# A hand-written order of 2159 steps, searched anew with copies tied to a load

## The chip, the cores and the metric

The kernel runs on one core of one Trainium2 chip. The metric is the device time of one execution in microseconds (us). The core's engines are TensorE (PE in the profile, its weight loads PEld), VectorE (DVE), ScalarE (ACT), GpSimd (POOL) and SyncE (SP), which here issues nearly all DMA transfers.

## What is computed

A recurrent attention with a decaying state, and behind it a gated product with a short convolution. Cut to what matters:

```python
# r, k, v, w: (4, 8, 768, 48) float32; u: (8, 48)
for t in range(S):
    cur = np.einsum('bhd,bhe->bhde', u[None] * kt, vt)
    y[:, :, t] = np.einsum('bhd,bhde->bhe', rt, state + cur)
    state = wt[:, :, :, None] * state + np.einsum('bhd,bhe->bhde', kt, vt)
# x: y as (4, 768, 384); w_in (384, 1024), w_out (1024, 384), three-row conv_w (float64)
h = np.maximum(x @ w_in, 0.0)
conv_out = sum(conv_w[j] * shifted(h, j - 1) for j in range(3))
out = (h * sigmoid(conv_out)) @ w_out
```

## The kernel before

The sequence is cut into 24 chunks of 128 times (four batches of six). For each chunk `loads` (L568) brings w, k and r into "nat" tiles and v into "v" tiles. TensorE transposes them, for chunks 8 to 23 in two rounds named 'f1' and 'f2' (L779). VectorE's scans (L645, L653) and products make the operands "kr". For chunks from 4 on, six small DMAs per chunk, the "spreads" (L674), lay out rows of kr for two more heads. `stage_b` (L716) computes scores, on TensorE, masks them (L795, VectorE) and forms the chunk's output y.

From chunk 8 on a chunk is split in two halves of 64 times. Its v goes by two loads (L581) into two of four v tiles, 64 rows each: the first tile holds v of the first half in rows 0 to 63, the second that of the second half in rows 64 to 127. The other rows of the same tiles take a copy of the state, so that one product yields what comes from inside the half and from the state before it: 'vsa' (L744) copies the decayed state into rows 64 to 111 of the first tile, 'vsb' (L885) the state at the half's boundary into rows 0 to 63 of the second. On TensorE the steps of such a chunk are 'hstate' (L877, needs v), 'hscores' (L763, kr), and 'hy' (L847, all of v, copies and scores); 'hy' is the last reader of a v tile, which is then free for a later chunk's load.

The eight blocks of 384 rows of the second part are on TensorE 'in' steps (L895, three matmuls each) and 'out' steps (L924, three each); between them ScalarE, VectorE and GpSimd form the gate (L907 to L917). ScalarE copies an output (L952) into a strip, SyncE sends it. The weights come in large loads and are converted on VectorE, ScalarE and GpSimd (L476 to L496) in the first 100 us.

Nothing of this is issued in the order of the code. Each step is noted by `op` (L187) with its engine, what it reads, what it writes and what buffers it holds. The list ORDER then gives the order in which `issue` (L205) emits the 2159 steps; each engine runs its own steps in this order. A negative number emits one warm-up matmul (L444) on a free bank. PLACES gives the buffer that a tile takes, at its first step. From what a step reads and writes `op` makes a set of steps that must be issued earlier; `issue` asserts it. Semaphores aren't set by it: they are derived from the memory that the emitted instructions touch.

The numbers of the steps that are spoken of:

| step | what it is |
|---|---|
| 696; 959, 1781, 1829 | y of chunk 7; 'hy' of chunks 10, 20, 21 |
| 788, 1162, 1990 | 'hstate' of chunks 9, 12, 22 |
| 723, 724; 938, 939; 986, 987; 1808, 1809; 1974, 1975 | loads of v, first and second half, of chunks 9, 11, 12, 22, 23 |
| 1146 to 1148; 1191 to 1193 | loads of w, k, r of chunks 13 and 14 |
| 969 to 974; 1134 to 1139; 2005 to 2010 | spreads of chunks 11, 12, 23 |

Of the kernel before, what the change touches and what calls it, by code (L numbers as in the profile page):

```python
# [28 lines left out]
    1, 5, 2, 49, 3, 212, 8, -6, 11, 219, 53, 50, 54, 10, 51, 258, 13, 52, 15, 180, 7, 6, 9, -8, -8, -8, -8, 19, 14,  # L29
    216, 220, 18, 16, 20, 23, 24, 173, 177, 181, 222, 25, 224, 183, 227, 0, 185, 214, 213, -5, -5, -5, 21, 217, 218,  # L30
    223, 228, 22, 165, 225, 188, 232, 26, 233, 166, 175, 174, 234, 167, 179, 251, 255, 259, 189, 229, 178, 190, 17,
    12, 4, 55, 226, 184, 186, 27, 29, 28, 170, 168, 236, 197, 230, 182, 221, 58, 193, 194, 195, 235, 196, 253, 252,
    261, 191, 169, 72, 66, 263, 73, 266, 257, 171, 172, 231, 198, 67, 256, 65, 56, 57, 192, 71, 199, 59, 237, 262,
    60, 267, 268, 61, 264, 242, 243, 203, 205, 215, 176, 30, 408, 271, 272, 74, 200, 68, 206, 207, 204, 201, 260,
    187, 69, 202, 269, 208, 273, 44, 415, 32, 38, 45, 33, 244, 209, 62, 63, 75, 239, 412, 31, 238, 270, 70, 451,
    409, 410, 210, 245, 416, 246, 254, 453, 452, 274, 76, 34, 432, 278, 433, 418, 211, 281, 282, 458, 37, 43, 240,
    413, 241, 455, 275, 414, 276, 35, 277, 420, 283, 247, 419, 459, 424, 248, 279, 457, 39, 461, 423, 434, 456, 265,
    280, 46, 463, 425, 421, 249, 284, 286, 287, 462, 467, 288, 47, 64, 77, 96, 250, 285, 289, 466, 464, 475, 476,
    40, 85, 477, 79, 468, 86, 436, 334, 335, 336, 345, 346, 347, 36, 48, 437, 438, 422, 417, 41, 84, 337, 338, 460,
    348, 349, 103, 429, 607, 431, 426, 428, 427, 430, 611, 647, 469, 609, 473, 608, 411, 470, 454, 472, 474, 471,  # L40
    115, 646, 42, 435, 87, 478, 301, 323, 312, 290, 615, 313, 302, 324, 325, 314, 291, 292, 303, 90, 88, 78, 439,
    616, 80, 89, 81, 104, 339, 105, 91, 350, 92, 351, 352, 340, 341, 110, 614, 353, 617, 342, 111, 442, 619, 98,
    622, 99, 444, 326, 315, 82, 445, 446, 443, 93, 83, 106, 441, 327, 94, 440, 109, 343, 112, 293, 95, 447, 328, 97,
    107, 316, 317, 479, 113, 354, 480, 612, 481, 304, 108, 294, 305, 114, 100, 631, 344, 632, 482, 367, 368, 369,
    448, 484, 483, 318, 329, 319, 306, 320, 295, 653, 485, 486, 613, 330, 331, 101, 720, 725, 449, 450, 650, 487,
    648, 134, 356, 357, 618, 623, 332, 122, 296, 488, 624, 297, 651, 298, 123, 321, 620, 358, 333, 355, 102, 322,
    654, 655, 359, 360, 511, 512, 299, 116, 370, 371, 489, 522, 490, 513, 514, 523, 491, 656, 124, 307, 117, 361,
    118, 125, 308, 670, 119, 300, 362, 676, 681, 363, 658, 372, 309, 373, 364, 661, 126, 120, 652, 524, 533, 534,
    535, 500, 501, 657, 536, 374, 365, 375, 502, 310, 128, 376, 135, 525, 621, 503, 121, 127, 662, 555, 556, 557,
    659, 129, 663, 130, 136, 137, 142, 633, 143, 675, 626, 610, 629, 677, 630, 678, 674, 366, 311, 131, 138, 377,  # L50
    537, 504, 492, 493, 132, 141, 144, 133, 538, 494, 539, 558, 559, 139, 540, 465, 140, 495, 505, 560, 496, 506,
    561, 679, 145, 515, 562, 507, 497, 516, 541, 526, 508, 563, 517, 146, 634, 671, 712, 713, 527, 672, 388, 389,
    390, 391, 392, 398, 399, 400, 401, 402, 393, 403, 404, 394, 405, 635, 395, 378, 379, 406, 636, 680, 509, 637,
    518, 519, 685, 686, 380, 688, 566, 567, 568, 381, 382, 383, 627, 668, 625, 669, 665, 667, 722, 721, 726, 564,
    727, 664, 666, 150, 628, 771, 528, 529, 498, 714, 700, 701, 704, 530, 702, 705, 396, 569, 690, 689, 570, 699,
    571, 572, 770, 573, 638, 732, 384, 385, 640, 733, 735, 639, 641, 649, 769, 693, 711, 708, 709, 710, 706, 707,
    574, 749, 642, 750, 753, 751, 542, 775, 510, 565, 673, 761, 762, 520, 521, 543, 682, 499, 386, 703, 736, 643,
    776, 774, 737, 644, 748, 531, 684, 683, 687, 544, 545, 546, 754, 927, 694, 729, 645, 692, 780, 781, 691, 740,
    783, 695, 696, 547, 548, 660, 723, 983, 988, 549, 763, 741, 915, 550, 916, 744, 919, 917, 920, 937, 942, 697,
    698, 551, 552, 575, 743, 784, 785, 914, 742, 758, 760, 756, 935, 755, 757, 759, 724, 936, 715, 532, 728, 764,  # L60
    718, 717, 719, 777, 765, 768, 716, 766, 984, 941, 778, 730, 940, 553, 985, 767, 554, 975, 976, 928, 576, 1140,
    587, 588, 589, 577, 578, 579, 788, 734, 782, 580, 789, 739, 792, 787, 590, 591, 738, 946, 779, 731, 745, 786,
    947, 790, 791, 746, 990, 752, 747, 793, 794, 949, 795, 963, 964, 965, 951, 950, 962, 989, 592, 593, 851, 967,
    977, 968, 929, 852, 594, 595, 853, 840, 994, 995, 841, 997, 807, 842, 808, 809, 407, 925, 922, 921, 923, 387,
    1192, 773, 1241, 854, 855, 856, 857, 1128, 858, 1129, 859, 1132, 843, 844, 845, 1130, 796, 797, 798, 581, 818,
    819, 820, 582, 583, 938, 926, 772, 930, 973, 1148, 924, 943, 934, 931, 933, 932, 987, 1240, 971, 970, 1146, 974,
    1147, 969, 596, 1133, 1139, 972, 810, 999, 1246, 846, 1137, 1135, 397, 1153, 811, 799, 800, 998, 1127, 847, 812,
    821, 801, 802, 848, 813, 1151, 803, 804, 954, 955, 958, 948, 918, 822, 953, 823, 952, 584, 1152, 945, 966, 957,
    814, 860, 585, 873, 874, 875, 876, 815, 1183, 991, 1184, 978, 979, 861, 1141, 982, 980, 981, 1154, 1155, 824,
    956, 877, 992, 825, 1002, 1157, 1003, 1171, 829, 862, 830, 863, 864, 831, 826, 816, 944, 959, 805, 1159, 1245,  # L70
    1158, 865, 866, 849, 1005, 1172, 878, 1173, 1175, 1142, 1176, 867, 879, 868, 832, 1197, 1004, 939, 1134, 1193,
    1138, 1182, 1191, 1136, 1181, 986, 993, 833, 869, 1170, 996, 597, 598, 599, 600, 601, 602, 603, 604, 1000, 834,
    870, 1001, 1185, 835, 817, 850, 960, 827, 828, 1143, 806, 1144, 1231, 1196, 880, 961, 881, 836, 1198, 837, 1232,
    1145, 1279, 1280, 1006, 1202, 1203, 1007, 1008, 1162, 1163, 1166, 605, 1205, 1156, 1219, 1220, 1223, 1221, 1224,
    1161, 1160, 1064, 1020, 1021, 1065, 1066, 1042, 1022, 1239, 1179, 1177, 1233, 1165, 1206, 1218, 1244, 1207,
    1164, 1067, 1288, 838, 1068, 1287, 882, 1293, 1250, 1167, 1251, 1253, 1168, 1254, 1131, 151, 1169, 1267, 1268,
    1269, 1271, 1255, 1222, 1023, 1024, 1043, 1044, 1009, 1053, 1054, 1055, 1010, 1069, 1272, 1031, 1011, 1289,
    1195, 1228, 1227, 1230, 1180, 1455, 1229, 1194, 586, 1178, 1454, 1226, 1453, 1278, 1225, 839, 1234, 871, 872,
    1186, 1045, 1292, 152, 1046, 1056, 1174, 1057, 1012, 1013, 1266, 1070, 1071, 1294, 1025, 1047, 1026, 1058, 1281,
    1014, 1072, 1059, 1048, 1015, 1032, 1075, 1033, 1076, 1034, 1077, 1027, 1459, 1060, 1049, 1460, 1078, 1035,  # L80
    1061, 1050, 1028, 1036, 1016, 1079, 1017, 1237, 883, 1236, 894, 895, 896, 897, 898, 899, 900, 1189, 901, 902,
    1235, 1190, 1188, 1277, 1275, 1274, 1150, 1149, 1210, 1273, 156, 606, 1276, 1199, 1187, 1037, 1211, 1080, 1214,
    1204, 1081, 1208, 1209, 1258, 1247, 1259, 1051, 1038, 1201, 1200, 1062, 1212, 1248, 1213, 1270, 1249, 1082,
    1039, 1083, 1262, 884, 885, 886, 887, 888, 1215, 1298, 1299, 1252, 1301, 889, 890, 891, 1040, 1216, 1018, 1260,
    1302, 1261, 1458, 1303, 892, 1063, 1445, 1243, 1502, 1503, 1501, 893, 1242, 1446, 1295, 1238, 1282, 1286, 1285,
    1284, 1283, 1052, 1019, 1447, 1217, 1256, 1257, 1433, 1434, 1437, 1435, 1438, 1432, 904, 905, 906, 1263, 1300,
    1464, 1264, 1296, 1507, 1508, 1304, 1305, 1465, 1265, 907, 1086, 908, 1467, 1306, 909, 910, 1087, 1088, 911,
    1084, 1480, 157, 1481, 1307, 1482, 1310, 1485, 1483, 1486, 1469, 1468, 1297, 1309, 1308, 1089, 1506, 1090, 1311,
    912, 1312, 1444, 1441, 1440, 1443, 1442, 1290, 1439, 1291, 1658, 1493, 1494, 1041, 1495, 1448, 1659, 1461, 1450,
# [938 lines left out]
```

## Time and profile before

| | us |
|---|---|
| median of three runs | 332.43 |
| the three runs | 331.68, 332.43, 334.64 |
| the profiled execution, its device time | 334.06 |
| its span, from the first to the last instruction | 331.9 |

The profiled execution is one of its own, not one of the three. Its device time is 2.2 us longer than the span that its trace covers. In the profile an engine's busy time is the union of its instructions; matmuls are pipelined and their ends modelled. A row of the timeline gives in brackets how long the engine was idle before it and what ended that. The chain of work that ended last is followed back from the last instruction; each of its pieces lies between one release and the next.

### The profile page before, as it was taken

The numbers are of one execution on the slowest core, as the hardware profiler recorded it, in microseconds if no ns is written. First come the engines' busy times: TensorE is split into PE (matmuls) and PEld (weight loads), VectorE is DVE, ScalarE is ACT, GpSimd is POOL, SyncE is SP. The second block draws the span as 40 slices with busy tenths as digits, with TensorE's granted clock in tenths as the row PEclk, the third lists the DMA queues.
The fourth block names the chain that finished last, engine by engine and source line by source line (L and its number), as shares of the span: only waits on it lengthen the run. The fifth ranks groups of instructions, "written<-read, shape, count | busy, mean of one in ns | idle before, by whom it ended". The sixth has DMA issues, their size and how long they took to land.

```text
span 331.9 us, 11314 instructions
## 1 busy us (share of the span) xinstructions
PE 315.7 (95%) x4450; PEld 292.6 (88%) x4450; DVE 258.9 (78%) x524; ACT 232.0 (70%) x621; POOL 207.3 (62%) x283
## 2 busy tenths in 40 slices
PE   7999999999999998799999999999999799999994
PEld 5887887989988997799988999998999699999994
DVE  5999998999996997768988997789878677554600
ACT  4458797998766588638966877877577578865531
POOL 5959998899786529645599661596384542334330
PEclk9999999999999999969999999999999899999999
DMA  7999769727555651454545664555416700000014
GB/s 152 247 231 212 246 131 227 178 51 196 106 100 119 139 121 32 93 112 95 147 120 115 136 173 102 149 152 114 83 35 196 200 8 2 2 0 1 2 71 148
DMA packets 114079, 39.36 MB, mean 119 GB/s; under 512 B 102605, under 2 KB 109542, under 8 KB 114022
## 3 DMA queue, kind: packets, MB, share of 16 engines
q1 hardware_dynamic: 114020, 38.59, 48.4%
q8 instruction: 36, 0.59, 0.8%
q14 instruction: 21, 0.17, 0.2%
q10 hardware_dynamic: 2, 0.00, 0.0%
HBM read 31.88 MB, written 4.72 MB: 110 GB/s over the span
## 4 chain that ended last, share of the span: by engine, by line
PE 56%; DVE 15%; DMA 11%; SPq 6%; ACT 5%; POOL 3%; issue 3%; DVEq 0%; ACTq 0%; POOLq 0%
PE bank L924 23%; PE bank L895 17%; PE bank L847 4%; SPq L674 4%; PE bank L779 4%; DMA nat<-in_k_dram 4%; DMA v<-in_v_dram 3%; DVE strip L911 3%; PE bank L763 3%; PE bank L877 3%; DVE strip L909 2%; DVE strip L914 2%; DMA gh<-in_moe_w_out_dram 2%; DMA kr<-kr 2%; DVE kr L645 1%
## 5 line engine op out<-in xcount | busy, mean ns | idle before, releaser
L895 PE MATMUL bank<-xT,wi 128*128 128x386 f32 x576 | 114.6, 349 | 0.2 <-DVE xT L856 0.2
L924 PE MATMUL bank<-wo,gh 128*128 128x384 f32 x576 | 109.2, 340 | 0.4 <-DVE strip L493 0.4
L895 PEld LDWEIGHTS bank<-xT,wi 128*128 128x128 f32 x576 | 103.4, 194 | 2.5 <-DVE xT L856 0.4
L917 POOL TENSOR_TENSOR gh<-strip,gh 128x384 fp32r<-128x384 f32 x64 | 64.9, 1023 | 63.1 <-ACT gh L916 54.2
L924 PEld LDWEIGHTS bank<-wo,gh 128*128 128x128 f32 x576 | 99.5, 188 | 2.0 <-DVE strip L493 0.7
L909 DVE SCALAR_TENSOR_TENSOR strip<-bank,cw,strip 128x384 f32<-128x384 f32 x64 | 38.4, 610 | 16.8 <-ACT strip L908 16.3
L913 ACT ACTIVATE strip<-strip 128x384 f32<-128x384 f32 x64 | 32.5, 522 | 20.5 <-DVE strip L911 20.0
L914 DVE TENSOR_TENSOR strip<-bank,strip 128x384 f32<-128x384 f32 x64 | 34.2, 552 | 8.0 <-ACT strip L913 7.9
L911 DVE SCALAR_TENSOR_TENSOR strip<-bank,cw,strip 128x384 f32<-128x384 f32 x64 | 38.3, 612 | 1.7 <-DVE strip L914 0.9
L908 ACT ACTIVATE strip<-bank,cw 128x384 f32<-128x384 f32 x64 | 36.5, 579 | 2.9 <-DMA out_dram<-strip 0.8
L795 DVE COPY_PREDICATED pm<-upper,bank 128x512 f32<-128x512 int32 x48 | 34.3, 736 | 2.9 <-PE bank L763 1.4
L907 ACT ACTIVATE bank<-bank 128x386 f32<-128x386 f32 x64 | 30.4, 478 | 8.1 <-PE bank L895 7.6
L916 ACT CAST gh<-strip 128x384 fp32r<-128x384 f32 x64 | 31.8, 508 | 3.8 <-DVE strip L914 2.6
L677 POOL TENSOR_TENSOR strip<-nat,nat 128x384 f32<-128x384 f32 x24 | 24.4, 1015 | 13.9 <-DMA out_dram<-strip 5.1
L683 POOL TENSOR_SCALAR_AFFINE_SELECT pm<-dg 128x1024 f32<-128x1024 f32 x24 | 26.7, 1113 | 9.3 <-DVE dg L680 4.8
L605 ACT COPY nat<-nat 128x96 f32<-128x96 f32 x72 | 18.5, 269 | 18.5 <-DMA nat<-in_w_dram 8.7
L692 POOL COPY pm<-kr 48x256 f32<-48x256 f32 x60 | 23.7, 395 | 6.4 <-DMA kr<-kr 3.5
L847 PE MATMUL bank<-pm,v 128*32 128x64 f32 (+3 forms) x1280 | 26.0, 231 | 0.6 <-POOL strip L679 0.6
L847 PEld LDWEIGHTS bank<-pm,v 128*32 128x32 f32 (+2 forms) x1280 | 22.2, 109 | 3.6 <-POOL strip L679 1.0
L679 POOL TENSOR_TENSOR strip<-strip,ubc 128x384 f32<-128x384 f32 x24 | 24.2, 1010 | 0.9
L645 DVE TENSOR_TENSOR_SCAN kr<-bank,one_end 128x387 f32<-128x387 f32 x24 | 23.0, 958 | 1.7 <-PE bank L779 0.8
L653 DVE TENSOR_TENSOR_SCAN kr<-bank,dA 128x387 f32<-128x387 f32 x24 | 23.0, 959 | 0.2
(105 smaller groups left out, 444.2 us busy)
## 6 DMA issues: line engine op xcount, KB each, us to landing
gh<-in_moe_w_out_dram SPq DMA_DIRECT2D x5, 1152.0 KB, 5.8
nat<-in_w_dram SPq DMA_DIRECT2D x24, 192.0 KB, 3.6
nat<-in_k_dram SPq DMA_DIRECT2D x24, 192.0 KB, 3.3
nat<-in_r_dram SPq DMA_DIRECT2D x24, 192.0 KB, 3.3
gh<-in_moe_w_in_dram SPq DMA_DIRECT2D x4, 1152.0 KB, 7.2
out_dram<-strip SPq DMA_DIRECT2D x24, 192.0 KB, 2.1
v<-in_v_dram SPq DMA_DIRECT2D x32, 96.0 KB, 3.1
kr<-kr SPq DMA_DIRECT2D x120, 16.1 KB, 2.4
```

What stands on the lines that cost most here:

```text
L795: op("DVE", "cp", lambda g=g: nc.vector.copy_predicated(out=pm.t[:, g], mask=upper.unsqueeze(1).to_broadcast([P, NP, L]), data=sc[g].t.rea ...
L847: nc.tensor.matmul(rows(a, 32)[:, ts], lhsT=lhs, rhs=rhs, start=((halved or c == 0) and i == 0), stop=(i == count - 1), skip_group_check=True)
L895: nc.tensor.matmul(t.t[:, 0:xs.stop - xs.start], lhsT=wi[:, m, a, f * P:(f + 1) * P], rhs=xT[:, x0 + m, c, xs], start=(m == 0 and j == 0), ...
L907: ("ACT", "relu", lambda: nc.scalar.activation(out=h(0, width + 2), in_=h(0, width + 2), func=AF.Relu), [t], [t]),
L908: ("ACT", "mul", lambda: nc.scalar.mul(out=a(), in_=h(1), mul=cw[:, 1, fs]), [t, "cw"], [a1]),
L909: ("DVE", "stt", lambda: nc.vector.scalar_tensor_tensor(out=a(), in0=h(0), scalar=cw[:, 0, fs], in1=a(), op0=ALU.mult, op1=ALU.add), [t], ...
L911: ("DVE", "stt", lambda: nc.vector.scalar_tensor_tensor(out=a(), in0=h(2), scalar=cw[:, 2, fs], in1=a(), op0=ALU.mult, op1=ALU.add), [t], ...
L913: ("ACT", "sig", lambda: nc.scalar.activation(out=a(), in_=a(), func=AF.Sigmoid), [], [a1]),
L914: ("DVE", "gate", lambda: nc.vector.tensor_tensor(out=g.t[:, 0:width], in0=h(1), in1=a(), op=ALU.mult), [t, a1], [g]),
L916: ("ACT", "cast", lambda: nc.scalar.copy(out=part(0)[:, 0:width], in_=g.t[:, 0:width]), [g], [key]),
L917: ("POOL", "lo", lambda: nc.gpsimd.tensor_tensor(out=part(1)[:, 0:width], in0=g.t[:, 0:width], in1=part(0)[:, 0:width].bitcast(F32), op=AL ...
L924: nc.tensor.matmul(acc.t[:, 0:DM], lhsT=part(a)[:, tt * P:(tt + 1) * P], rhs=wo[:, f, c, :], start=(f == 0 and a + c == 0), stop=(f == FT ...
```

## The change

ORDER and PLACES are replaced as a whole. ORDER has the same 2159 steps in another order and 29 warm-up matmuls instead of 8; all of the 29 stand ahead of the output product of chunk 5. Two steps change in what they are noted to read: the copies 'vsa' and 'vsb' now read the v tile that they write into, where they only held its buffer before. Cut to the core, with those lines of ORDER in which the steps spoken of stand (each line is one of many):

```diff
 ORDER = [
...
-    783, 695, 696, 547, 548, 660, 723, 983, 988, 549, 763, 741, 915, 550, 916, 744, 919, 917, 920, 937, 942, 697,
...
-    1147, 969, 596, 1133, 1139, 972, 810, 999, 1246, 846, 1137, 1135, 397, 1153, 811, 799, 800, 998, 1127, 847, 812,
...
-    956, 877, 992, 825, 1002, 1157, 1003, 1171, 829, 862, 830, 863, 864, 831, 826, 816, 944, 959, 805, 1159, 1245,
-    1158, 865, 866, 849, 1005, 1172, 878, 1173, 1175, 1142, 1176, 867, 879, 868, 832, 1197, 1004, 939, 1134, 1193,
-    1138, 1182, 1191, 1136, 1181, 986, 993, 833, 869, 1170, 996, 597, 598, 599, 600, 601, 602, 603, 604, 1000, 834,
...
-    1540, 1541, 1781, 1829, 1582, 1583, 1429, 1584, 1959, 1411, 1962, 1957, 1960, 1958, 159, 2007, 1421, 2010, 2006,
-    2005, 2008, 1809, 1961, 2009, 1782, 1783, 1576, 1577, 1830, 1542, 1578, 1602, 1585, 1586, 1831, 1543, 1544,
-    1430, 1843, 2019, 2021, 1545, 2020, 1876, 1877, 1878, 1844, 1845, 1974, 1808, 1990, 1966, 1537, 2014, 1979,
...
+    521, 762, 573, 531, 532, 687, 643, 693, 692, 691, 695, 696, 547, 644, 548, 748, 752, 574, 697, 694, 763, 645,
...
+    863, 864, 1241, 1159, 939, 1004, 956, 959, 1158, 993, 876, 1175, 1176, 865, 1005, 866, 1131, 877, 1170, 823,
...
+    1964, 1965, 1543, 1586, 1827, 1574, 2019, 1781, 1829, 1782, 1830, 2020, 1426, 1427, 1428, 1429, 1961, 1960,
+    1957, 162, 1958, 1421, 2008, 1959, 2010, 2007, 2006, 1962, 1809, 1808, 2005, 1974, 2009, 2021, 1587, 1588, 1783,
...
 ]
...
                     op("ACT", "vsa", lambda g=g, p=p: nc.scalar.copy(
-                        out=vN[0].t[HL:HL + D, :, 64 * g:64 * g + D], in_=sd.t[p]), [sd], [(vN[0], 1 + g)], [vN[0]])
+                        out=vN[0].t[HL:HL + D, :, 64 * g:64 * g + D], in_=sd.t[p]), [sd, vN[0]], [(vN[0], 1 + g)])
...
             op("ACT", "vsb", lambda g=g: nc.scalar.copy(
-                out=vN[1].t[0:64, :, 64 * g:64 * g + D], in_=mid.t[64 * g:64 * g + 64]), [mid], [(vN[1], 1 + g)], [vN[1]])
+                out=vN[1].t[0:64, :, 64 * g:64 * g + D], in_=mid.t[64 * g:64 * g + 64]), [mid, vN[1]], [(vN[1], 1 + g)])
```

SyncE's own queue, taken out of the two lists at the places spoken of (v, nat and spread with the chunk's number):

| place | before | after |
|---|---|---|
| from the first to the last load of v 9 | v 9 (723), nat 12, nat 11, three spreads 9, nat 11, three spreads 9, v 9 (724) | v 9 (723), two spreads 9, v 9 (724) |
| around load 939 | v 11 (939), spread 12, nat 14, spreads 12 and 13, nat 14, spreads 12 and 13, v 12 (986) | v 11 (939), spread 12, output, spread 12, nat 14, spread 12, nat 14, spread 12, nat 14, output, two spreads 13, nat 15, spread 12, v 12 (987), v 12 (986) |
| around load 1808 | v 22 (1809), spreads 22 and 23, v 23 (1974), v 22 (1808) | v 22 (1809), v 22 (1808), spread 23, v 23 (1974) |

Load 939 takes the v tile that 'hy' of chunk 10 frees in the order before, the tile that 'hy' of chunk 9 frees in the order after. The two loads of chunk 12 wait for 'hy' of chunk 10 in the order after, those of chunk 22 both for 'hy' of chunk 20; before, 1808 waits for 'hy' of chunk 21.

## Rows read from the trace of the kernel before

**Rows 1.** The page, its first part: busy us, share of the span, instructions

```profile
PE 315.7 (95%) x4450; PEld 292.6 (88%) x4450; DVE 258.9 (78%) x524; ACT 232.0 (70%) x621; POOL 207.3 (62%) x283
```

**Rows 2.** Stretches: length, busy us (instructions) per engine, granted clock, DMA share, GB/s

```profile
9.00:100.00 91.00, 87.75 (x1215) 78.93 (x1214) 88.00 (x181) 71.14 (x203) 80.34 (x94) 1.00 0.72 174
100.00:164.00 64.00, 59.80 (x960) 55.21 (x961) 52.10 (x103) 45.64 (x128) 37.23 (x53) 0.95 0.48 100
164.00:250.00 86.00, 85.60 (x1485) 79.58 (x1479) 72.69 (x143) 62.99 (x173) 55.81 (x76) 1.00 0.50 122
250.00:268.00 18.00, 15.94 (x338) 15.06 (x331) 13.68 (x27) 10.98 (x25) 9.02 (x15) 0.91 0.65 183
```

**Rows 3.** Timeline of TensorE: start, us, what [idle before it <- what ended that]

```profile
102.06 0.61 PE L877 MATMUL bank<-v,kh 64*64 64x48 f32 x26 [0.82 <-DMA v<-in_v_dram]
...
126.00 0.27 PE L779 MATMUL bank<-ident,kr 64*128 64x64 f32 x1 [1.44 <-ACT strip L952]
...
139.74 0.27 PE L779 MATMUL bank<-ident,nat 64*128 64x64 f32 x1 [1.33 <-ACT nat L605]
...
140.69 1.11 PE L877 MATMUL bank<-v,kh 64*64 64x48 f32 x32 [0.37 <-DMA v<-in_v_dram]
...
261.71 0.72 PE L877 MATMUL bank<-v,kh 64*64 64x48 f32 x30 [2.06 <-DMA v<-in_v_dram]
```

**Rows 4.** Stretches behind two of these waits, columns as in rows 2

```profile
141.00:147.00 6.00, 6.00 (x86) 5.67 (x80) 5.01 (x10) 2.04 (x7) 3.23 (x4) 0.50 0.65 128
...
263.00:267.00 4.00, 4.00 (x55) 3.88 (x51) 4.00 (x9) 0.93 (x2) 1.81 (x5) 0.57 0.61 199
```

**Rows 5.** Chain that ended last: start, us, what, at half and full clock

```profile
140.69 1.11 PE bank L877 x32
...
143.69 5.55 PE bank L895 x21
...
184.17 0.62 PE bank L877 x32
185.30 5.51 PE bank L895 x30
...
257.73 3.94 DMA v<-in_v_dram
...
264.21 8.84 PE bank L895 x42
```

**Rows 6.** Timeline of SyncE's issues, 119 to 138 us

```profile
124.90 0.58 SPq L953 DMA_DIRECT2D out_dram<-strip  x1
132.24 0.64 SPq L581 DMA_DIRECT2D v<-in_v_dram  x1
...
137.47 0.64 SPq L581 DMA_DIRECT2D v<-in_v_dram  x1
```

**Rows 7.** Timeline of SyncE's issues, two later places

```profile
174.71 0.64 SPq L581 DMA_DIRECT2D v<-in_v_dram  x1
...
256.97 1.38 SPq L581 DMA_DIRECT2D v<-in_v_dram  x2
```

**Rows 8.** Timeline of ScalarE, two rows

```profile
123.41 0.27 ACT L605 COPY nat<-nat 128x96 f32<-128x96 f32 x1 [1.35 <-DMA nat<-in_k_dram]
...
176.30 0.35 ACT L744 COPY v<-sd 48x192 f32<-48x192 f32 x1
```

**Rows 9.** Loads of v by halves (L581): from issue to landing

```profile
DMA to landing us min/median/max: 2.6/3.1/4.4
```

**Rows 10.** Warm-up matmuls (L444): duration ns min/median/max, first and last start

```profile
L444 PE MATMUL bank<-ident x8: 393/421/421, 3.7 to 9.6; 128*128 128x256 bf16 x8
```

**Rows 11.** Chain that ended last: durations of other steps at full clock

```profile
113.53 0.53 PE bank L779 x12
...
168.15 1.03 PE bank L847 x64
...
206.54 5.74 PE bank L924 x33
```

251 rows, old and new, of tables (ORDER, PLACES) are left out of this document.

## The prediction, made before the change was run

> **What bounds the kernel now.** I read the page's first part, then the busy time by stretches, the idle time in front of TensorE's instructions, the chain of work that ended last, and the SyncE queue in order of time. TensorE is busy 95% of the span, VectorE 78% [rows 1]. The stretches tell two regimes apart. From 9 to 100 us VectorE is busy 88.00 of 91 us: weights are converted there, and TensorE's own busy time (87.75) is no evidence against that, since few instructions (1215) fill it with modelled ends [rows 2]. From 100 us on TensorE leads: it is idle 4.2 us of 100 to 164, 0.4 of 164 to 250 and 2.06 of 250 to 268 [rows 2]. So what a new order can win lies in few places after 100 us.
>
> Five waits on TensorE's row name them: 0.82 at 102.06 for a load of v, 1.44 at 126.00 for a copy on ScalarE, 1.33 at 139.74 for the fill of a loaded tile, 0.37 right after it and 2.06 at 261.71 for loads of v [rows 3]. Together 6.02 us. Behind the third and the fifth the granted clock is 0.50 and 0.57 [rows 4], the lower of the two levels in part or whole, and the same work is longer: 21 matmuls of L895 took 5.55 us where 30 take 5.51 at full clock (0.184 each, so 3.86 for 21: 1.7 lost), 32 of L877 took 1.11 instead of 0.62 (0.5 lost), and 42 of L895 took 8.84 instead of 7.7 (1.1 lost) [rows 5]. That is 3.3 us. All told 9.3 us.
>
> Why they waited is seen on SyncE, which issues every load in one queue. After an issue at 124.90 it issues nothing until 132.24, where a load of v goes out; the next load of v goes at 137.47 [rows 6]. By the order of the steps the load at 132.24 is 939 (second half of chunk 11, into a tile that hy[10] frees), and the one at 137.47 is 986 (first half of chunk 12), eight issues behind. The loads of nat for chunk 14, whose fill the transposes at 139.74 wait for, sat between the two. The later place is of the same kind: the two loads of v from 256.97 on are step 1974 (chunk 23) and behind it 1808 (chunk 22) [rows 7]; the chain has 1808 from its issue at 257.73 for 3.94 us [rows 5], and TensorE starts on it at 261.71 [rows 3]. The wait at 126.00 goes back to ScalarE, which stood 1.35 us before a fill at 123.41 for a landing of nat [rows 8], k of chunk 13.
>
> **The change, part by part.** The two edits in the code put a step's number among what must be issued before the copies 'vsa' and 'vsb'. The kernel's own plan uses this for the assertion on the order alone; semaphores come from the memory that instructions touch. Rows that a copy writes are not those that the load writes: the copy of chunk 15 at 176.30 began 1.6 us after the issue of its tile's load at 174.71, below the shortest landing of such loads, 2.6 [rows 7 to 9]. So I cost the edits at nothing; if they did make copies wait (the rival below), ScalarE would stand until a landing, 2.6 to 4.4 less 1.6, which is 1.0 to 2.8 us for this copy.
>
> The order of 2159 steps is new. The steps are the same but for 29 warm-up matmuls instead of 8. All 29 stand ahead of the outputs of chunk 5 in TensorE's queue, in the part where weights are converted and VectorE is the limit. One shows 421 ns [rows 10], so they cost between 0 (covered by VectorE's work) and 21 x 0.42 = 8.8 us (if TensorE were the limit there); I take 0, since TensorE has the slack, and if VectorE's cover were gone the upper end would count.
>
> Ahead of the first halved state products ('hstate' of chunk 9) the new queues hold 195 VectorE instructions instead of 192, by counting everything that must come before. At 88.00 us for 181 instructions [rows 2] the three cost 1.5 us there. Bounds: no cost, if they fill the 3 us that VectorE is idle in that stretch, or a gain up to those 3 us; against that 1.5 more, were the three exposed twice by the handing over to ScalarE. I take 1.5.
>
> SyncE's queue: each new place is worked out from TensorE's work between the step that frees the tile and the step that reads it. Per step: 'in' or 'out' of three matmuls 0.55 and 0.52, 'hy' 1.03, 'hstate' 0.62, 'f1' or 'f2' 0.53, and 'hscores', with as many small matmuls, taken as 'hstate' [rows 5, 11]; an issue 0.64 [rows 6]; a landing 3.1, at most 4.4 [rows 9]. Chunk 9: after y[7] come f1, hstate, f2, seven out and two hscores, 6.5 us, against one issue and a landing, 3.7: covered, and 0.82 goes. Chunk 12: 987 and 986 are now adjacent and behind the nat loads of chunk 14, 939 takes a tile that hy[9] frees; after hy[10] come hscores, three in, eight out, hy and f1, 8.0 us, against two issues and a landing, 4.4: the 1.33 and 0.37 and their clock go. Chunk 22: both halves now wait for hy[20] alone and are adjacent; hy, four out and five in, 5.9 us, against 4.4: the 2.06 and its clock go, with 1.5 to spare, or 0.2 at the slowest landing. The 1.44: the load of k of chunk 13 (1147) stood behind four of the six spreads of chunk 11 and now stands ahead of all six, so I count it as gone, with none of it gone as the other end. Removed: 9.3 us.
>
> What is late next? The same sum at the other chunks is thinnest for 16 (6.4 us against three issues and a landing, 5.0), 18 (7.8 against five, 6.3) and 20 (5.7 against one, 3.7). All have 1.4 to 2.0 us to spare, and 0.1 to 0.7 at a landing of 4.4. Behind each load that waits at the queue's head stand spreads whose readers are 'hscores' and the copies on GpSimd; from the first to the last spread of a chunk the new queue has 181 issues in all over chunks 8 to 23, the old 203. Both say that stalls become rarer, not that there is none. I charge one of the kind seen, 2.06 and 1.1 for its clock, 3.2 us; ends are 0 and three of the larger kind (1.70 and 2.2, 3.9 each).
>
> On landings there is a rule that speaks against the change. The slowest v load took 4.4, the median one 3.1 us [rows 9]. The Trainium skill, "DMA: Bandwidth & Descriptors", section "Anatomy of one DMA — SWDGE (gpsimd) path", fits about 2.0 us plus bytes over 436 GB/s; by that estimate the 96 KB land in 2.2 us, and planning for later landings buys nothing (by it the time would stay at 332.4). The trace's landings differ from it, on SyncE's queue, which is not that path.
>
> The sum: -9.3 + 1.5 + 3.2 = -4.6 us. The profiled execution took 334.06 us (span 331.9, 2.2 around it); the median of the runs is 332.43, 1.63 below it. 334.06 - 4.6 = 329.5, and on the median's footing 327.8 us.
>
> **The rivals.** First: the stalls only move. For it speaks that one queue issues all loads, spreads and outputs, twelve a chunk, so that something always stands behind a waiting load; against it the sums above. Then -9.3 + 9.3 + 1.5 gives 333.9 us: no change. The rule on landings would end here too.
>
> Second, the slower side: SyncE's queue runs behind at the thin places (chunks 16, 18, 20, 22). There a load must be at the queue's head when 'hy' ends; late spreads or an output issue ahead of it push it beyond what it has to spare, and TensorE waits long enough to lose the clock, 3.9 us each. Two of them give -9.3 + 1.5 + 7.8 = 0, 332.4; from the third on it is slower by over 1%: 336.3. For it: both drops of before came in this way. Against it: the new queue is shorter between spreads.
>
> Third: the copies do wait for the landing. At chunks like 15 ScalarE, busy 70% [rows 1], would stand 1.0 to 2.8 us and products behind it too; at two such chunks 2 x 2.8 = 5.6 over the sum, 333.4: no change. The copy at 176.30 speaks against it.
>
> **How the numbers follow.** The forecast (net gain of more than 1%) has 0.60, moved stalls 0.20, the queue that runs behind 0.13 (0.04 of it at two stalls, 0.09 at three or more), waiting copies 0.03, and 0.04 for warm-ups or VectorE work that are exposed at their upper ends (327.8 + 8.8 = 336.6). About 1% is what a measurement of this kernel can tell from no change. Faster 0.60, same 0.27 (0.20 + 0.04 + 0.03), slower 0.13. The forecast's own range is 321 to 329: all of the 9.3 with nothing charged is 334.06 - 9.3 - 1.63 = 323.1, and with VectorE's 3 us of idle time used it is 320.1; 321 leaves little out. The other cases reach to 336.6; the top is set at 335.5, which leaves the 0.13 of the slower cases outside, and the bottom a few hundredths.
>
> **What would show it.** Right: no wait for v in front of L877 over 0.5 us, granted clock 1.00 from 100 us to the end, no gap in SyncE's row like 124.90 to 132.24, TensorE idle under 3 us from 100 to 268. VectorE's busy share up to 100 us stays above 90%, and the state products of chunk 9 are at work by 103 us. Wrong: waits of 1 us and more at chunks 13 to 22 with a clock below 1.00 behind them, a load of v that goes out late though its tile is free, idle time on VectorE before 100 us, or copies of L744 that begin right at a landing.

## The result and the profile after

| | us |
|---|---|
| changed kernel, median of four runs | 324.11 (323.45 to 325.21) |
| kernel before, four runs beside them | 333.26 (331.68 to 334.64) |
| ratio, 95% interval | 0.973 (0.967 to 0.979) |
| profiled execution of the changed kernel, its span | 322.4 (before 331.9) |

The kernel is 9 us faster. Its time is 3.7 us below the 327.8 that was forecast and inside the forecast's own range of 321 to 329; the gain is 9.15 us, where the sum had 4.6. Ratios here leave out runs more than 1.5% above the fastest of their kernel, while the medians further down are over all runs, so that for kernels whose times scatter the two can differ by some tenths of a per cent. Line numbers of the changed kernel are one higher than before from L445 on (L878 is 'hstate', L582 the half load of v, L925 'out').

Busy time, and the granted clock by 40 slices:

```profile
PE 313.7 (97%) x4471; PEld 290.4 (90%) x4471; DVE 260.6 (81%) x524; ACT 230.3 (71%) x621; POOL 206.7 (64%) x283
...
PEclk9999999999999999999999999999999999999999
```

The stretches, columns as in [rows 2]:

```profile
9.00:100.00 91.00, 89.50 (x1234) 81.33 (x1233) 87.65 (x183) 68.94 (x200) 80.56 (x96) 1.00 0.70 171
100.00:164.00 64.00, 63.44 (x1128) 58.40 (x1129) 57.32 (x115) 51.68 (x145) 42.27 (x59) 1.00 0.55 125
164.00:250.00 86.00, 85.67 (x1488) 79.73 (x1489) 72.04 (x141) 62.72 (x173) 53.22 (x74) 1.00 0.51 123
250.00:268.00 18.00, 17.97 (x202) 17.56 (x201) 15.51 (x27) 13.80 (x32) 10.63 (x15) 1.00 0.40 107
```

TensorE is idle 0.56, 0.33 and 0.03 us in the last three, 0.92 in all, where it was 6.66 before [rows 2], and the clock is 1.00 in all three instead of 0.95, 1.00 and 0.91. Of the five waits of [rows 3] one has an heir, at chunk 12 (timeline of TensorE):

```profile
137.74 0.79 PE L878 MATMUL bank<-v,kh 64*64 64x48 f32 x32 [0.51 <-DMA v<-in_v_dram]
```

SyncE's row at the places of [rows 6, 7], and from issue to landing of the half loads of v, as in [rows 9]:

```profile
131.68 2.11 SPq L675 DMA_DIRECT2D kr<-kr  x1
133.92 3.00 SPq L582 DMA_DIRECT2D v<-in_v_dram  x3
...
247.25 1.77 SPq L582 DMA_DIRECT2D v<-in_v_dram  x2
...
DMA to landing us min/median/max: 2.5/2.8/5.8
```

The two halves of chunk 12 now go out one after the other, at 133.92 and 134.69 (the third load of that row is one of chunk 13), those of chunk 22 likewise from 247.25 on. The chain of work that ended last shows both places: at chunk 12 it still runs over a spread and the load of v, at chunk 22 it stays on TensorE:

```profile
129.78 2.25 DMA kr<-kr
...
134.69 2.91 DMA v<-in_v_dram
...
137.74 0.79 PE bank L878 x32
...
250.37 2.66 PE bank L896 x15
253.02 0.61 PE bank L878 x32
```

### The profile page after: what moved, and what is told of

Same layout as the page of the kernel before. It is cut to its first block, busy times and chain, and to the rows that moved or that the text cites. A ratio compares the mean times of both kernels' runs of the same rounds, so it can differ in the third digit from the quotient of the medians.

```text
span 322.4 us, 11370 instructions
## 1 busy us (share of the span) xinstructions
PE 313.7 (97%) x4471; PEld 290.4 (90%) x4471; DVE 260.6 (81%) x524; ACT 230.3 (71%) x621; POOL 206.7 (64%) x283
## 4 chain that ended last, share of the span: by engine, by line
PE 81%; DVE 7%; DMA 5%; ACT 2%; SPq 1%; issue 1%; DVEq 0%; ACTq 0%
PE bank L925 28%; PE bank L896 27%; PE bank L848 6%; PE bank L780 5%; PE bank L878 3%; PE bank L764 3%; DMA gh<-in_moe_w_out_dram 2%; PE bank L632 2%; PE bank L756 2%; PE bank L666 1%; DVE strip L910 1%; DMA nat<-in_k_dram 1%; DVE strip L912 1%; DVE bank L491 1%; DVE strip L915 1%
## 5 line engine op out<-in xcount | busy, mean ns | idle before, releaser
L896 PE MATMUL bank<-xT,wi 128*128 128x386 f32 x576 | 113.2, 344 | 0.1
L925 PE MATMUL bank<-wo,gh 128*128 128x384 f32 x576 | 108.3, 340 | 0.4 <-DVE strip L494 0.4
L896 PEld LDWEIGHTS bank<-xT,wi 128*128 128x128 f32 x576 | 100.4, 189 | 2.2 <-DVE strip L494 0.3
L925 PEld LDWEIGHTS bank<-wo,gh 128*128 128x128 f32 x576 | 99.8, 188 | 1.7 <-DVE strip L494 0.7
L953 ACT COPY strip<-bank 128x384 f32<-128x384 f32 x24 | 11.3, 477 | 17.3 <-PE bank L925 17.3
```

Source lines behind the costliest of these rows:

```text
L896: nc.tensor.matmul(t.t[:, 0:xs.stop - xs.start], lhsT=wi[:, m, a, f * P:(f + 1) * P], rhs=xT[:, x0 + m, c, xs], start=(m == 0 and j == 0), ...
L925: nc.tensor.matmul(acc.t[:, 0:DM], lhsT=part(a)[:, tt * P:(tt + 1) * P], rhs=wo[:, f, c, :], start=(f == 0 and a + c == 0), stop=(f == FT ...
```

## The experiments

Twelve kernels ran. The diffs of ORDER are cut to the steps that move.

### The changed kernel once more

No edit: the changed kernel as it is.

> The changed kernel itself, timed in as many rounds as its variants beside it, so that they can be set against it. Theory (its loads land before TensorE asks for them, so that a landing a little later costs nothing): the times lie close together, within 2.5 us of each other, about 324, 0.973 of the kernel before. Rival (its profile was one lucky execution): the times spread by 6 us and more, as those of the kernel before, with a ratio nearer to 0.985.

Median 324.39 us, six runs from 323.69 to 326.91 (a span of 3.2, a little over the 2.5 expected); ratio 0.9725 (0.968 to 0.977); the kernel before had 334.54 beside it. TensorE is idle 0.83 us from 100 to 268 in this profile, so the first one was not a lucky execution. The wait at chunk 12 is 0.17 here:

```profile
137.24 0.79 PE L878 MATMUL bank<-v,kh 64*64 64x48 f32 x32 [0.17 <-ACT xT L856]
```

The load lands 0.14 us before it ends, so it is still this load that TensorE starts on. The variants of the changed kernel are set against 324.39.

### The two edits alone

```diff
-    1158, 865, 866, 849, 1005, 1172,
+    1158, 865, 866, 849, 939, 1005, 1172,
...
-    832, 1197, 1004, 939, 1134, 1193,
+    832, 1197, 1004, 1134, 1193,
...
-                        out=vN[0].t[HL:HL + D, :, 64 * g:64 * g + D], in_=sd.t[p]), [sd], [(vN[0], 1 + g)], [vN[0]])
+                        out=vN[0].t[HL:HL + D, :, 64 * g:64 * g + D], in_=sd.t[p]), [sd, vN[0]], [(vN[0], 1 + g)])
...
```

> The kernel before with the two edits in the code alone; one step's place in the list moves so that the load it names stands ahead of the copy, and every engine keeps its own order. Theory (the order does all of it, the edits set no wait on the chip): the time of before, within 1 us, and the copies of L744 do not begin right at a landing. Rival (the copies do wait for the load): ScalarE stands 1 to 2.8 us at a copy, and the time is 1 us or more above that of before.

Medians 334.60 against 334.36, ratio 1.0076 (1.003 to 1.012). In the profile no idle time of ScalarE ends in front of the copies of L744, as none did before. So the rows speak for the theory. The times don't decide: the medians are 0.2 us apart, while the ratio puts this kernel 2.5 us higher (1.1 to 4.0), which is what the rival asked for, though its engines run the same instructions in the same order. Whether that is chance or real was not settled, and a difference below 0.8% between kernels of the old order is not shown to be an effect. What the profile does show is how the old order changes from execution to execution. The waits of TensorE (compare [rows 3]):

```profile
102.08 0.61 PE L877 MATMUL bank<-v,kh 64*64 64x48 f32 x26 [1.03 <-DMA v<-in_v_dram]
109.67 0.54 PE L847 MATMUL bank<-pm,v 128*32 128x64 f32 x22 [2.00 <-issue]
142.26 0.27 PE L779 MATMUL bank<-ident,nat 64*128 64x64 f32 x1 [1.38 <-ACT nat L605]
261.38 0.72 PE L877 MATMUL bank<-v,kh 64*64 64x48 f32 x30 [1.32 <-DMA v<-in_v_dram]
```

The 1.44 at 126 is not among them, a wait of 2.00 inside 'hy' of chunk 9 is new, and the other sizes differ. "issue" says that no releaser is seen.

### The place of chunk 12 mended in the old order

```diff
-    934, 931, 933, 932, 987, 1240,
+    934, 931, 933, 932, 939, 1240,
...
-    832, 1197, 1004, 939, 1134, 1193,
+    832, 1197, 1004, 1134, 1193,
...
-    1138, 1182, 1191, 1136, 1181, 986, 993,
+    1138, 1182, 1191, 1136, 1181, 987, 986, 993,
```

In PLACES the tiles of 939 and 987 change over, and those of the later loads with them.

> The kernel before with one place of SyncE's queue mended: load 939 (second half of v, chunk 11) goes early into the tile that 'hy' of chunk 9 frees, so that nothing stands behind it while 'hy' of chunk 10 is awaited, and the two loads of v of chunk 12 go out one after the other. Theory (each stall in the queue costs its wait and the half clock behind it): the waits of 1.33 and 0.37 us in front of TensorE at 140 us go, and so does the 0.50 of the granted clock behind them, 2.2 us: 3.9 us less than before (-3 to -5). Rival 1 (the stall only moves): within 1 us of before, with a new wait at chunk 13 or 14. Rival 2 (only the wait counts, and the clock falls anyway): 1.7 us less.

Median 333.76 against 334.36, ratio 1.0034 (0.999 to 1.008): nothing gained, so the theory's 3.9 us did not come. The wait at chunk 12 is down to 0.64 and the clock is 1.00 from 100 to 164 us, but TensorE stands elsewhere:

```profile
139.99 0.79 PE L877 MATMUL bank<-v,kh 64*64 64x48 f32 x32 [0.64 <-DVE xT L856]
...
161.09 0.73 PE L877 MATMUL bank<-v,kh 64*64 64x48 f32 x30 [1.12 <-DVE strip L911]
...
266.26 6.41 PE L895 MATMUL bank<-xT,wi 128*128 128x386 f32 x26 [1.99 <-issue]
```

'hstate' of chunk 22 starts at 259.1 instead of 261.7; the 2.6 us are lost again behind it, with the wait at 266.26 and a clock of 0.80 from 263 to 270. Rival 1 held. The wait at 161.09 goes back to SyncE once more, since the later half of v lands 0.14 us before it ends (the named releaser is an earlier one). SyncE's row shows the loads of v of chunk 13 behind a train of issues with no gap, the last five of them spreads:

```profile
153.97 3.13 SPq L674 DMA_DIRECT2D kr<-kr  x5
157.15 1.37 SPq L581 DMA_DIRECT2D v<-in_v_dram  x2
```

### The place of chunk 22 mended in the old order

```diff
-    2005, 2008, 1809, 1961,
+    2005, 2008, 1809, 1808, 1961,
...
-    1844, 1845, 1974, 1808, 1990,
+    1844, 1845, 1974, 1990,
```

> The kernel before with the other place mended alone: load 1808 (second half of v, chunk 22) stands right behind 1809 and takes the tile that 'hy' of chunk 20 frees; load 1974 (chunk 23) takes its old place and tile. Theory: the wait of 2.06 us at 261.7 and the 1.1 us of half clock behind it go: 3.2 us less than before (-2.5 to -4). Rival 1 (the stall moves to chunk 23, whose load is now the later one): within 1 us of before, with a wait at chunk 23. Rival 2 (only the wait counts): 2.1 us less.

Median 330.85 against 334.36, which is 3.5 less; the ratio is 0.9948 (0.990 to 0.999), 1.7 us of 333, and smaller than the 0.8% named above. The wait of 2.06 is gone, and TensorE is not idle from 250 to 268 us, though the profiled execution is the slowest of the twelve (334.74 us). The sign is the theory's. The size is not settled: the interval, 0.2 to 3.3 us, holds the theory's 3.2 and the 2.1 of rival 2, and it reaches down to rival 1. Little work that another engine could hold up comes behind this place: the state products of chunk 23 are the last.

### Four places mended in the old order

The edits of the two kernels above, and besides:

```diff
-    760, 756, 935, 755, 757, 759, 724, 936,
+    760, 756, 935, 724, 755, 757, 759, 936,
...
-    973, 1148, 924, 943,
+    973, 1148, 1146, 1147, 924, 943,
```

with 1146 and 1147 taken from their old places.

> The kernel before with four places of SyncE's queue mended and nothing else: those of chunk 12 and of chunk 22, the loads of nat for chunk 13 ahead of the spreads of chunk 11, and the second load of v of chunk 9 ahead of three spreads. Theory (these four places are what the new order wins, and the rest of the 2159 steps in new places is worth nothing): 9.3 us less than before, which is the time of the changed kernel within 1.5 us. Rival (the rest of the order carries a good part of it): 4 to 7 us less than before, and 2 us or more above the changed kernel.

Median 330.53, ratio 0.9884 (0.984 to 0.993): 3.9 us of 333 (2.2 to 5.5), not 9.3. The rival held: these four places are about four tenths of the gain. New waits stand where the old ones were (the profiled execution took 332.33 us, so the sizes are those of a longer one):

```profile
105.62 0.27 PE L779 MATMUL bank<-ident,kr 64*128 64x64 f32 x1 [1.19 <-DVE pm L795]
109.26 0.54 PE L847 MATMUL bank<-pm,v 128*32 128x64 f32 x22 [1.19 <-issue]
140.80 0.79 PE L877 MATMUL bank<-v,kh 64*64 64x48 f32 x32 [0.99 <-DMA v<-in_v_dram]
163.37 0.77 PE L877 MATMUL bank<-v,kh 64*64 64x48 f32 x30 [0.93 <-DMA v<-in_v_dram]
262.60 0.57 PE L877 MATMUL bank<-v,kh 64*64 64x48 f32 x13 [1.56 <-DVE strip L909]
```

The last two end with a landing of v as well. The first is the instructive one: the load of chunk 9 is early now, its 0.82 is gone, and TensorE waits 1.19 us for the masks on VectorE (L795) instead, as it does in the two other profiles with that load early (1.18 and 1.20).

### All loads of v placed by one rule

```diff
-    816, 944, 959, 805, 1159,
+    816, 944, 959, 986, 987, 805, 1159,
...
```

Chunk 12 stands for chunks 10 to 23, whose loads leave their old places; 724 as in the kernel above.

> The kernel before with the loads of v alone placed anew: from chunk 10 on both halves of chunk n stand right behind 'hy' of chunk n-2 and take the two tiles that it frees, and the second load of chunk 9 stands ahead of three spreads; all other steps keep their order. By TensorE's work that leaves 6.3 us and more from the freeing to the reader at chunks 10 to 23. Theory (what is left over the four mended places is the other loads of v that land just as their reader starts, at chunks 13, 16, 19 and 23): 7 to 10 us less than before, the time of the changed kernel within 2 us. Rival 1 (the spreads and loads of nat behind them, and waits that no load of v explains, carry the rest): 3 to 5 us less than before, no better than the four places alone. Rival 2 (loads that wait in groups of four block the spreads behind them): no gain or a loss, with waits of TensorE in front of scores.

Median 359.66, ratio 1.068 (1.061 to 1.075): about 23 us slower by the ratio. Rival 2 held, and far beyond the loss that I had in mind. The loads themselves are as early as wanted: from issue to the 'hstate' that reads them the shortest is 3.2 us and the middle one 14.3, against 3.0 and 8.1 in the changed kernel. But they go out in groups of four, and a group waits at the head of SyncE's queue for its last tile. SyncE's row at chunks 16 and 17, and two of TensorE's waits:

```profile
180.57 9.21 SPq L581 DMA_DIRECT2D v<-in_v_dram  x4
189.88 4.59 SPq L674 DMA_DIRECT2D kr<-kr  x6
...
197.00 6.03 PE L895 MATMUL bank<-xT,wi 128*128 128x386 f32 x21 [4.66 <-DVE sd L881]
...
286.56 0.45 PE L763 MATMUL bank<-kr 48*64 48x64 f32 x2 [5.45 <-DMA kr<-kr]
```

Six spreads follow the 9.21 us of the group, and what they bring is waited for: by scores directly (5.45 us at 286.56), by GpSimd's copies of the state (POOL sd L736 waits for kr 32.5 us in all) and by what hangs on them. An early load of v is worth nothing if the spreads pay for it.

### The place of chunk 12 put back in the new order

```diff
-    863, 864, 1241, 1159, 939, 1004, 956, 959, 1158,
+    863, 864, 1241, 1159, 956, 959, 939, 1004, 1158,
```

The tiles of 939 and 987 change over in PLACES, and those of the later loads with them. SyncE issues in the same order as in the changed kernel; what is put back is the 'hy' that load 939 waits for. On ScalarE one copy (956) comes ahead of another (1004).

> The changed kernel with one place of SyncE's queue put back as it was: load 939 (chunk 11) stands behind 'hy' of chunk 10 and waits for its tile, and 987 takes the tile that 'hy' of chunk 9 frees; the loads of nat for chunk 14 and the first load of v of chunk 12 are behind the waiting one. Theory: TensorE waits for them at 137 to 142 us and the granted clock falls behind it, 3.9 to 6 us more than the changed kernel. Rival 1 (the rest of the new order has slack for it): within 1 us of the changed kernel. Rival 2 (the wait comes, but the clock stays at 1.00): 1.5 to 3 us more.

Median 331.90, twelve runs from 330.95 to 332.61: 7.5 us above the changed kernel, where 3.9 to 6 were expected. The mechanism is the theory's, at nearly twice the lower end of its size. SyncE issues nothing from 122.3 to 128.5, when 'hy' of chunk 10 has freed the tile, and then has fourteen issues, the waiting load the first of them, ahead of the loads of chunk 12:

```profile
121.86 0.45 SPq L574 DMA_DIRECT2D nat<-in_r_dram  x1
128.50 0.65 SPq L582 DMA_DIRECT2D v<-in_v_dram  x1
...
137.52 2.89 SPq L582 DMA_DIRECT2D v<-in_v_dram  x3
```

TensorE's wait for them, and the stretch behind it:

```profile
142.33 1.22 PE L878 MATMUL bank<-v,kh 64*64 64x48 f32 x32 [3.92 <-DMA v<-in_v_dram]
...
141.00:147.00 6.00, 4.67 (x81) 4.37 (x82) 3.08 (x6) 2.15 (x7) 1.93 (x3) 0.54 0.43 104
```

'hstate' of chunk 12 starts 4.6 us later than in the changed kernel's profile (142.3 against 137.7), that of chunk 13 7.1 later (157.8 against 150.7): 2.5 us more at the lower clock. The end is 6.9 later (spans 329.3 and 322.4). So nothing behind chunk 13 gives it back, and nothing is added. The stall is not the old one over again: in the order before the late load was eight issues behind the waiting one and TensorE waited 1.33 and 0.37 us [rows 3], here the two loads are fourteen and fifteen behind, and TensorE waits 3.92.

### The changed kernel without warm-ups

```diff
-    1, 2, 173, 49, 3, 175, 212, 180, 10, 5, -7, -7, -7, -7, 11, 13,
+    1, 2, 173, 49, 3, 175, 212, 180, 10, 5, 11, 13,
...
```

and so on for all 29.

> The changed kernel without its 29 warm-up matmuls on a free bank (they compute nothing that is used). Theory (VectorE sets the first 100 us, so that TensorE's extra work there costs and gives nothing): within 1 us of the changed kernel. Rival 1 (they stand on the path): up to 8 us less (29 x 0.273). Rival 2 (they keep the clock up): 1 us or more longer, with a granted clock below 1.00 in the first 50 us.

Median 323.15 against 324.39, ratios 0.9676 (0.964 to 0.972) and 0.9725 (0.968 to 0.977), whose intervals overlap: no loss, and a gain of 1.2 us by the medians and 1.6 by the ratios that is not certain. TensorE idles 7.6 us in the first 100, where it is 3.7 with the warm-ups; 'hstate' of chunk 9 starts 0.8 us later for it (103.8 against 103.0), that of chunk 12 no later (137.7 in both). The clock is 1.00 without them as well, from the first 10 us on. So the theory held but for some tenths beyond its 1 us, and both rivals fail. It is the lowest median of all that ran.

### Two loads more in the old order

The first kernel is the mended chunk 12, the second the four places, both with this:

```diff
-    1228, 1227, 1230, 1180, 1455,
+    1228, 1227, 1230, 1180, 1149, 1150, 1455,
...
-    1277, 1275, 1274, 1150, 1149, 1210,
+    1277, 1275, 1274, 1210,
```

> The kernel before with the place of chunk 12 mended and, besides, both loads of v of chunk 13 moved ahead of eleven issues: SyncE sent those eleven back to back, 0.64 us each, ahead of the two loads (157.2 and 157.9), though 'hy' of chunk 12 had freed the tiles at 147.6. Theory (the mended stall of chunk 12 was lost again at chunk 13, whose loads the queue reaches late): the wait of 1.12 us in front of the state products of chunk 13 at 161 goes, and the time is 2 to 4 us below before, where the mended chunk 12 alone gave 0.6. Rival 1 (the queue only passes the delay on to the spreads behind): within 1 us of the mended chunk 12 alone. Rival 2 (the stalls come from late landings at random places, and no two mended places bring anything): within 1 us of before.

> The kernel before with the four mended places and, as the fifth, the two loads of v of chunk 13 ahead of eleven issues. Theory (each thin place that is mended hands its gain to the next thin one, until none is left): 1 to 2.5 us below the four places alone, 5 to 6.5 us below before, with the rest of the way to the changed kernel in waits for VectorE at chunk 9 and for v at chunks 12 and 23. Rival (nothing more is had from the loads of v): the time of the four places, 3.8 us below before, within 0.7.

With chunks 12 and 13: median 333.66 against 335.23, ratio 0.9976 (0.993 to 1.002). That is less than the theory's 2 to 4 us and can't be told from nothing, though the wait at 161 is gone. Both rivals forecast that, and this kernel alone does not part them. With five places: median 329.31, ratio 0.9818 (0.975 to 0.988), 6.1 us of 333 and 2.2 below the four places. That agrees with the theory, but the intervals of the two overlap. What is left of the way, seen in the five places:

```profile
100.00:164.00 64.00, 58.89 (x1026) 54.25 (x1026) 52.70 (x106) 46.51 (x129) 37.38 (x52) 1.00 0.51 112
...
104.70 0.27 PE L779 MATMUL bank<-ident,kr 64*128 64x64 f32 x1 [1.20 <-DVE pm L795]
109.10 0.54 PE L847 MATMUL bank<-pm,v 128*32 128x64 f32 x22 [1.96 <-issue]
133.81 4.45 PE L924 MATMUL bank<-wo,gh 128*128 128x384 f32 x24 [0.65 <-DVE kr L657]
163.28 2.87 PE L924 MATMUL bank<-wo,gh 128*128 128x384 f32 x15 [0.80 <-DVE sd L881]
```

TensorE is idle 5.1 us from 100 to 164, where the changed kernel has 0.56. The spans differ by 4.8 (327.2 and 322.4). So with the loads of v mended the rest sits in waits for VectorE's masks, operands and states, and in one of 1.96 us inside 'hy' that has no releaser (the last section comes back to it). The new order moved those steps too; which of these moves counts was not tried.

### VectorE lengthened, early and late

```diff
-        op("DVE", "dg", lambda: nc.vector.tensor_reduce(
-            out=dg.t.rearrange("p (g m) -> p m g", g=2), in_=z.t.rearrange("p (m g) d -> p m g d", g=2), axis=AX.X,
-            op=ALU.add), [z], [dg])
+        def reduced():
+            for _ in range(2 if 2 <= n < 8 else 1):
+                nc.vector.tensor_reduce(
+                    out=dg.t.rearrange("p (g m) -> p m g", g=2), in_=z.t.rearrange("p (m g) d -> p m g d", g=2), axis=AX.X,
+                    op=ALU.add)
+        op("DVE", "dg", reduced, [z], [dg])
```

The second kernel has 14 <= n < 20 instead.

> The changed kernel with one short reduction on VectorE (0.545 us, the same result twice) done twice in chunks 2 to 7: six more instructions, 3.3 us, all before 100 us. Theory (VectorE sets the time of the first 100 us): 2.5 to 3.3 us more than the changed kernel. Rival (TensorE sets it, or the 3 us in which VectorE is idle take it): within 1 us of the changed kernel.

> The changed kernel with the same reduction done twice in chunks 14 to 19: six more instructions, 3.3 us, all behind 100 us. Theory (TensorE sets the time there, and what VectorE makes comes early enough): within 1 us of the changed kernel. Rival (the order is so tight that a later product on VectorE delays SyncE's spreads and with them the loads behind): 2 us or more above it, with a new wait of TensorE and a clock below 1.00 behind it.

Early: median 327.44 (327.18 to 327.70), 3.05 above 324.39, of 3.3 us added. Late: 324.84, 0.45 above, inside the scatter of the changed kernel. Both theories held: up to 100 us VectorE sets the time, and behind it VectorE has room, while TensorE is busy 97 to 100% of the stretches there. One and the same output product in the changed kernel and in the early variant (three lines more of code):

```profile
74.65 7.04 PE L925 MATMUL bank<-wo,gh 128*128 128x384 f32 x39 [0.39 <-DVE strip L494]
```

```profile
78.63 7.06 PE L928 MATMUL bank<-wo,gh 128*128 128x384 f32 x39 [0.98 <-DVE strip L494]
```

It starts 4.0 us later; what it waits for comes from VectorE in both.

## Why the prediction was right, and where it was not

**The mechanism.** The prediction said that the gain lies in few waits of TensorE behind 100 us, that their cause is a load waiting at the head of SyncE's queue, and that a lower clock behind two of them adds half as much again. The trace of after bears out the place: idle time from 100 to 268 us fell by 5.74 us (forecast 6.02), and the clock rose to 1.00 in the two stretches that had 0.95 and 0.91 (forecast 3.3 us). The sum forecast was 9.3, the spans differ by 9.5. Of the other signs promised, VectorE is busy 87.65 of 91 us up to 100, and the state products of chunk 9 are at work at 103.0. Two came only in part: the wait for v at chunk 12 is just over the 0.5 allowed, and SyncE's row still has a gap of 5.1 us, from 232.2 to 237.3 ahead of a spread, behind which TensorE does not wait. The kernel with chunk 12 put back shows the cause in the new order: one load behind 'hy', and 7.5 us are lost through a chain of this kind, with a longer wait than the old one.

**The step that was mis-sized** is the pair of charges, 4.7 us, for things that come late next. The stall charged with 3.2 us came as 0.51 at chunk 12 (0.17 in the second profile, none without the warm-ups), with no loss of clock. And it came where I had not looked: I had named chunks 16, 18, 20 and 22 as the thin ones and counted chunk 12 as safe with 3.6 us to spare. The sum there ran from the freeing of the tile, and SyncE's queue reaches the load only at 133.9, about 5 us after 'hy' of chunk 10 is through (it starts at 127.9), because it has issues almost without a gap from 121.3 on, one of which, the spread at 131.68, takes 2.11 us. A load that goes out late though its tile is free was a sign that the prediction had put under wrong; it is the mechanism of the second rival, at another place and for half a microsecond. For its price, had it come in full, 3.2 may have been too low: the kernel with chunk 12 put back paid 7.5 for a wait of 3.92.

**The charge of 1.5 and the 0.82 at chunk 9** cancel, and neither reached the end. 'hstate' of chunk 9 starts 2.1 us later than before (103.0 against 100.9), so the charge was right in sign, and the wait behind it is gone; but 'hy' of chunk 9 starts at 107.1 against 106.8. The masks on VectorE set this point: the four mended places turned the 0.82 into a wait of 1.19 for them. I had booked a wait as a gain with another engine's work right behind it.

**What was put at nothing** was nothing. The warm-ups: without them the time is the same or up to 1.6 us less, far from the 8.8 of the upper end, since VectorE carries the first 100 us, which the lengthened reductions show directly. The edits: no copy waits for a load.

**The rivals.** That stalls only move was wrong for the whole order, but right for chunk 12 alone: mending it in the old order gave nothing, while in the new order its undoing, with a longer stall, costs most of the gain. The profiles of the old order with one to five places mended still have 6.1 to 8.6 us of idle TensorE from 100 to 268 us, the kernel before 6.7. That the waits can be added up place by place, on which the sum rests, is therefore not borne out: the five waits were not five causes. Their sum came out because the new order mends the loads, the spreads behind them and VectorE's order together. That last step is concluded from the waits that stayed, not shown by a kernel of its own. It does not cover all of them either: of what stayed, 1.96 us with five places and 1.99 with chunk 12 mended are waits without a releaser, which end shortly after a packet of the queue for instructions (last section), and the new order has none of that size.

**Landings.** By the Trainium skill, "DMA: Bandwidth & Descriptors", section "Anatomy of one DMA — SWDGE (gpsimd) path", a half load would land in an estimated 2.2 us. By the prediction's reading of it, planning for later landings would then bring nothing. The half loads on SyncE's queue, which is not that path, landed in 2.5 to 5.8 us, the middle one in 2.8, and the time fell by 9 us. The measurement decides; how much of the gain is owed to the allowance for late landings as such was not separated.

## What to carry to other kernels

A load that waits for its buffer at the head of an in-order queue delays everything behind it, so place it by when the queue reaches it and by what stands behind it, not by how early it could go: the rule that sent all loads early cost about 23 us. Waits read off one execution can be added up only if nothing else is nearly as late; before counting a wait as a gain, look at what each other engine finishes at the same point. To learn what a place is worth, undo it in the better kernel as well as mending it in the worse one: here the first gave 7.5 us and the second nothing. Compare the two stalls before comparing the prices, since the undone one need not be as long as the old one.

## What had not been expected of the hardware

The fall of the granted clock does not follow the length of a wait. Before, 1.33 and 0.37 us were followed by 0.50 [rows 3, 4]; with the five places, waits of 1.20 and 1.96 us between 103 and 109 left it at 1.00; with the edits alone a wait of 2.00 at the same 'hy' was followed by 0.72:

```profile
104.00:112.00 8.00, 5.24 (x163) 4.81 (x164) 4.18 (x9) 4.16 (x13) 6.20 (x7) 1.00 0.27 74
```

```profile
109.00:115.00 6.00, 5.33 (x50) 5.16 (x50) 4.09 (x8) 1.94 (x6) 2.15 (x3) 0.72 0.34 65
```

What tells them apart stays open.

Six of the seven profiled variants of the old order have a wait inside 'hy', of 0.7 to 2.0 us, for which the profile names no releaser, each ahead of the same matmul, the 107th of the 128 of chunks 8 and 9; the profile of the kernel before has none there, nor has any of the new order. A second one, of 1.3 to 2.0 us, is at 264 to 268 us in three of them (1.99 with chunk 12 mended). One thing in the trace goes with them: the queue that the page lists as 'q8 instruction', which moves 36 packets of 16 KB. With the edits alone its part of the profile from 107.2 to 108.2 us is (packets, MB, share of the 16 DMA engines)

```profile
q8 instruction: 1, 0.02, 5.8%
```

That packet ends at 108.19 and TensorE goes on at 109.67; with chunk 12 mended a packet ends at 264.92 and TensorE goes on at 266.26. All ten waits of 0.6 us and more without a releaser behind 100 us, over all the profiles, end 1.2 to 1.5 us after the end of such a packet. That TensorE stood there for its own instructions is the nearest reading; no kernel moved such a packet, so it is not shown.

One half load of v, the last, lands late in the changed kernel: 5.8 us, in other executions of the new order 6.5 and 7.7, where the slowest had taken 4.4 before [rows 9]; it has over 9 us to spare.
